# Second layer: seven block products for two f-tiles by two chunks of tokens, in place of eight

## The chip, the cores and the metric

The kernel runs on one core of a Trainium2 chip. The metric is device time in microseconds, from the profile's clock of one launch; the median of the runs is what counts. The engines are called as the profile calls them: PE (TensorE, matrix products), PEld (its weight loads), DVE (VectorE), ACT (ScalarE), POOL (GpSimd) and SP (SyncE, which only starts transfers here).

## What is computed

An attention in which a query sees the keys of its own hash bucket gives 1536 tokens of 512 values. Two feed-forward layers follow; the second one is what the change is about. The weights are float64 in memory, the activations float32.

```python
def _moe_ref(x, w1, w2, w3, w_out):            # first layer, d_ff 1024
    return ((x @ w1) * (x @ w2) @ w3) @ w_out

def _moe2_ref(x, w_gate, w_val, w_out):        # second layer, d_ff 1536
    gate = 1.0 / (1.0 + np.exp(-(x @ w_gate)))
    val = x @ w_val
    return (gate * val @ w_out).astype(np.float32)
```

## The kernel before

Attention, the decoding of the float64 weights and the first layer's first chunk fill the first 390 us or so. The rest is `moe` (L771). It works on tiles `(layer, chunk, f-tile)`: a chunk is 512 tokens (`CH`), of which there are three (`NSW`); an f-tile is 128 of the hidden values, 8 in the first layer (`NF1`), 12 in the second (`NF2`). The list `tiles` (L774) has the first layer's chunks two and three, then the second layer's chunks one, two and three.

Every product of float32 operands is made of three matmuls in a fast format: each operand is split into a high part, a rounded copy made by ACT, and a low part, the rest, made by a subtraction on DVE or POOL; `three` (L753) multiplies high by high, high by low and low by high into one bank of PSUM. `stage1` (L759) does so for the four blocks of 128 of the contraction, so a first product of a tile, `[128 hidden values x 512 tokens]`, is twelve matmuls into one bank.

For each tile:

- `weights` (L780) splits the gate's and the value's 512 x 128 block of weights, two tiles ahead: high parts on ACT, low parts on POOL (`split_w`, L741; tiles `wa`, `wb`).
- the first products go to the banks `pa` (gate) and `pb` (value), two of each.
- `post` (L788): ACT takes the sigmoid of `pa` into `a`, DVE multiplies `pb` by it in place, ACT and DVE split the result into `gh` and `gl`.
- `second` (L802), one tile late: the second product, twelve matmuls, adds to the four banks `m0` to `m3`, which hold 512 tokens by 512 outputs over all f-tiles of a chunk. At the chunk's end ACT (or DVE) copies the banks to `o` and SP stores them.

The operands that move through PE in the first products are the split activations: `xh`, `xl` for chunk one, and two pairs of tiles `x2_0_1`, `x2_1_1` (named `x` in the profile) for chunks two and three. The float32 weights of all f-tiles lie in SBUF, decoded, in `xall` and in the first layer's old tiles (`ftile`, L763). The float64 weights are decoded (`decode`, L136, on ACT, POOL and DVE) up to some 575 us.

The order of the instructions on each engine in `moe` comes from a scheduler that follows the code's priorities, with a wait for whoever wrote an operand or still reads a buffer.

Of the kernel before, what the change touches and what calls it, by code (L numbers as in the profile page):

```python
# [11 lines left out]
F32 = mybir.dt.float32  # L12
F32R = mybir.dt.float32r
# [5 lines left out]
AF = mybir.ActivationFunctionType  # L19
ALU = mybir.AluOpType  # L20
# [268 lines left out]
def lsh_attention_moe_moe2_kernel(  # L289
# [68 lines left out]
    wc = big.tile([P, NF1, DM], F32, name="wc")  # L358
# [377 lines left out]
    def split_x(s, t, kcs):  # L736
        for kc in kcs:
            act_copy(t[0][:, kc], xraw[s][:, kc])
            dve.tensor_tensor(out=t[1][:, kc], in0=xraw[s][:, kc], in1=f(t[0][:, kc]), op=ALU.subtract)

    def split_w(pl, nm, src, bufs=2, eng=pool):  # L741
        hi = pl.tile([P, DM], F32R, tag=nm + "h", name=nm + "h", bufs=bufs)
        lo = pl.tile([P, DM], F32R, tag=nm + "l", name=nm + "l", bufs=bufs)
        shp = src.shape
        h3, l3 = hi, lo
        if len(shp) == 3:
            h3 = hi.rearrange("p (k f) -> p k f", k=shp[1])
            l3 = lo.rearrange("p (k f) -> p k f", k=shp[1])
        act_copy(h3, src)
        eng.tensor_tensor(out=l3, in0=src, in1=f(h3), op=ALU.subtract)  # L750
        return hi, lo

    def three(ps, lhs, rhs, start, stop):  # L753

        for n, (x, y) in enumerate(((0, 0), (0, 1), (1, 0))):
            mm = pe.matmul(ps, lhsT=lhs[x], rhs=rhs[y], start=start and n == 0, stop=stop and n == 2)  # L756
        return mm

    def stage1(ps, w, x, kcs):  # L759
        for kc in kcs:  # L760
            three(ps, [t[:, kc * P:(kc + 1) * P] for t in w], [t[:, kc] for t in x], kc == 0, kc == KC - 1)

    def ftile(fi):  # L763

        ck, o = divmod(fi, KC)
        g = xall[:, o, ck * CH:(ck + 1) * CH].rearrange("p (k f) -> p k f", k=KC)
        if fi < NF1:
            return g, late["w1"][fi], late["w2"][fi].rearrange("p k f -> p (k f)")
        return g, wc[:, fi - NF1].rearrange("p (k f) -> p k f", k=KC), wc[:, fi - NF1 + KC]

    def moe(psM):  # L771
# [15 lines left out]

        def post(n, ps):  # L788
            m, s, fi = tiles[n]
            a = mp.tile([P, CH], F32, tag="a", name="a", bufs=2)  # L790
            if m == 1:
                act_copy(a, ps[0])
            else:
                act.activation(out=a, in_=ps[0], func=AF.Sigmoid)
            gl = mw.tile([P, CH], F32R, tag="gl0", name="gl", bufs=2)
            dve.tensor_tensor(out=ps[1], in0=ps[1], in1=a, op=ALU.mult)  # L796
            gh = mw.tile([P, CH], F32R, tag="gh0", name="gh", bufs=2)
            act_copy(gh, ps[1])
            late["gl"] = dve.tensor_tensor(out=gl, in0=ps[1], in1=f(gh), op=ALU.subtract).ins
            return gh, gl  # L800

        def second(n, g, wt, acc):  # L802
            m, s, fi = tiles[n]
            nf = NF1 if m == 1 else NF2
            last = n == len(tiles) - 1
            mm = None
            for c in range(4):
                cs = slice(c * P, (c + 1) * P)
                with tc.issue_after(mm.ins) if last and c else nullcontext():
                    if m == 1:  # L810
                        mm = three(acc[c], [t[:, cs] for t in wt], g, fi == 0, fi == nf - 1)
                    else:
                        mm = three(acc[c], [t[:, cs] for t in g], wt, fi == 0, fi == nf - 1)
            if fi < nf - 1:
                return
            for c in range(4):
                if m == 1:
                    act_copy(x2[s][0][:, c], acc[c])
                    dve.tensor_tensor(out=x2[s][1][:, c], in0=acc[c], in1=f(x2[s][0][:, c]), op=ALU.subtract)
                else:  # L820
                    o = mp.tile([P, DM], F32, tag="a" if last and c < 2 else "o", name="o", bufs=2)
                    if last and c % 2:
                        dve.tensor_copy(o, acc[c])
                    else:
                        act_copy(o, acc[c])
                    b, n = divmod(s * (CH // P) + c, NT)
                    sync.dma_start(out=out[b * S:(b + 1) * S].rearrange("(p c) d -> c p d", c=NT)[n], in_=o)
# [4 lines left out]
        for n in range(len(tiles) + 1):
            if n < len(tiles):
                ps = [psM.tile([P, 512], F32, tag=t, name=t) for t in ("pa", "pb")]
                x = x2[tiles[n][1]]
                w = ops.pop(n)
                for kcs in ([range(KC)] if n else [range(KC - 1), range(KC - 1, KC)]):
                    for i in range(2):
                        stage1(ps[i], w[i], x, kcs)
                m, s, fi = tiles[n]  # L840
                wts[n] = split_w(mp, "wt", wc[:, fi] if m == 1 else ftile(fi)[2], eng=dve)
                gs[n] = post(n, ps)
            if n == 0:
                continue
            if acc is None:
                acc = [psT.tile([P, 512], F32, tag="t", name="m0"), psT.tile([P, 512], F32, tag="t", name="m1"),
                       psT.tile([P, 512], F32, tag="t", name="m2"), psT.tile([P, 512], F32, tag="t", name="m3")]
            second(n - 1, gs.pop(n - 1), wts.pop(n - 1), acc)
# [15 lines left out]
    o = D // 2  # L864
# [12 lines left out]
    for r, c in ((slice(0, D), 0), (slice(D, P), o)):  # L877
        hi, lo = (t[r, c:c + NB] for t in pq)
# [43 lines left out]
    done = [0, 0.0]  # L922
# [85 lines left out]
```

## Time and profile before

| | |
|---|---|
| runs | 804.04, 804.48, 806.04 us (median 804.48) |
| profiled execution | 806.79 us; span of its instructions 805.0 us |
| granted clock of PE | 0.998 on average over the span |
| PE busy | 781.3 us, 97% of the span, 4016 matmuls |
| PEld | 661.1 us (82%) |
| DVE, ACT, POOL busy | 470.9 us (59%), 511.4 us (64%), 434.2 us (54%) |

A line of a group names the source line, engine, operation, output and inputs, shapes and how often, then the busy time and the mean of one. The line of a helper stands for all its callers (`act_copy` is L335). The chain of waits is the sequence of work that ended last, followed back from the last instruction. "Idle before" is how long the engine stood still in front of an instruction, with what released it behind the arrow.

### The profile page before, as it was taken

How to read it: one execution, taken by the hardware profiler on the slowest of the kernel's cores; microseconds unless marked ns; L12 is line 12 of the kernel's file. 1: busy time of each engine (PE TensorE's matmuls, PEld its weight loads, DVE VectorE, ACT ScalarE, POOL GpSimd, SP SyncE). 2: the span in 40 equal slices, each digit the busy share in tenths (PEclk: the TensorE clock that was granted, in tenths of full speed). 3: DMA queues.
4: the chain of work that ended last, by engine and by line, in shares of the span. 5: the costliest groups of instructions: out<-in, count | busy, mean ns of one | idle time of the engine just before them, and what ended most of it. 6: DMA issues, size and time to landing. Idle time of an engine off the chain costs nothing.

```text
span 805.0 us, 11532 instructions
## 1 busy us (share of the span) xinstructions
PE 781.3 (97%) x4016; PEld 661.1 (82%) x4016; DVE 470.9 (59%) x722; ACT 511.4 (64%) x946; POOL 434.2 (54%) x459
## 2 busy tenths in 40 slices
PE   6899899999899999999999999999999999999998
PEld 4789798899788899988888888888888888888886
DVE  6989988876997889782654445664422222222222
ACT  6889997877998888873555557766434333343332
POOL 6758886655675654494455557767423233332320
PEclk9999999999999999999999999999999999999999
DMA  9956676544366543230031213433001000010001
GB/s 278 223 160 151 187 197 180 145 123 117 117 163 167 135 126 102 69 106 0 27 105 53 79 53 116 141 110 105 0 1 53 0 1 1 0 53 1 0 1 53
DMA packets 28505, 74.46 MB, mean 92 GB/s; under 512 B 6048, under 2 KB 8352, under 8 KB 28448
## 3 DMA queue, kind: packets, MB, share of 16 engines
q1 hardware_dynamic: 28368, 73.73, 31.8%
q8 instruction: 32, 0.52, 0.3%
q14 instruction: 25, 0.20, 0.1%
q10 hardware_dynamic: 80, 0.00, 0.0%
HBM read 52.82 MB, written 3.19 MB: 70 GB/s over the span
## 4 chain that ended last, share of the span: by engine, by line
PE 84%; ACT 7%; POOL 3%; DVE 2%; issue 2%; DMA 2%; SPq 0%; ACTq 0%; POOLq 0%; DVEq 0%
PE m L756 18%; PE pa L756 18%; PE pb L756 18%; PE av L596 6%; PE tp L578 5%; PE p L756 5%; PE wacc L651 4%; PE s L526 3%; PE s L529 3%; PE y L756 2%; ACT e L545 2%; ACT pt L581 2%; PE gps L447 2%; DMA st<-in_moe_w_dram 1%; DVE sm L535 1%
## 5 line engine op out<-in xcount | busy, mean ns | idle before, releaser
L796 DVE TENSOR_TENSOR pb<-pb,a 128x512 f32<-128x512 f32 x52 | 36.3, 699 | 178.4 <-PE pb L756 178.4
L750 POOL TENSOR_TENSOR wal<-xall,wah 128x512 fp32r<-128x512 f32 x36 | 46.9, 1304 | 107.4 <-ACT wah L335 107.4
L583 DVE TENSOR_TENSOR pt<-tp,pt 128x512 fp32r<-128x512 f32 x144 | 94.9, 682 | 9.6 <-ACT pt L581 8.8
L578 PE MATMUL tp<-idf,e 128*128 128x128 f32 x576 | 95.8, 274 | 4.8 <-ACT e L545 2.3
L756 PE MATMUL pa<-x,wah 128*128 128x512 f32 x320 | 99.8, 391 | 0.0
L756 PE MATMUL pb<-x,wbh 128*128 128x512 f32 x320 | 98.8, 389 | 0.0
L398 POOL TENSOR_SCALAR dr<-st 128x512 bf16<-128x512 f32 x76 | 72.9, 971 | 45.8 <-issue 21.2
L535 DVE TENSOR_REDUCE sm<-s 128x1 f32<-128x768 f32 x96 | 90.3, 948 | 12.1 <-PE s L529 10.1
L545 ACT ACTIVATE e<-s,sm 128x768 f32<-128x768 f32 x96 | 86.7, 906 | 10.5 <-DVE sm L535 8.5
L581 ACT ACTIVATE pt<-tp 128x512 fp32r<-128x512 f32 x144 | 82.7, 599 | 9.3 <-PE tp L578 7.6
L578 PEld LDWEIGHTS tp<-idf,e 128*128 128x128 f32 x576 | 71.7, 141 | 15.7 <-ACT e L545 3.4
L596 PE MATMUL av<-pt,spv 128*128 128x256 f32 x576 | 80.3, 286 | 2.1 <-DVE pt L583 1.3
L596 PEld LDWEIGHTS av<-pt,spv 128*128 128x128 f32 x576 | 74.5, 190 | 5.2 <-DVE pt L583 2.5
L756 PEld LDWEIGHTS pa<-x,wah 128*128 128x128 f32 x320 | 60.1, 188 | 13.5
L756 PEld LDWEIGHTS pb<-x,wbh 128*128 128x128 f32 x320 | 60.1, 188 | 12.7
L399 POOL TENSOR_SCALAR da<-da 128x512 f32<-128x512 f32 x76 | 49.8, 663 | 37.2 <-ACT da L396 33.6
L526 PE MATMUL s<-bk,bq 128*128 128x384 f32 x192 | 61.2, 376 | 5.3 <-ACT e L545 4.9
L651 PE MATMUL wacc<-wo,t 128*128 128x512 f32 x192 | 61.9, 410 | 1.2 <-POOL wo L646 0.9
L756 PE MATMUL pa<-x,wal 128*128 128x512 f32 x160 | 62.4, 390 | 0.0
L756 PE MATMUL pb<-x,wbl 128*128 128x512 f32 x160 | 62.3, 389 | 0.0
L397 ACT ACTIVATE dr<-st 128x512 int16<-128x512 uint32 x76 | 60.1, 794 | 0.0
L529 PE MATMUL s<-ak,aq 128*128 128x384 f32 x192 | 58.7, 366 | 0.0
(146 smaller groups left out, 1823.2 us busy)
## 6 DMA issues: line engine op xcount, KB each, us to landing
st<-in_moe_w_dram SPq DMA_DIRECT2D x32, 512.0 KB, 5.3
st<-in_moe_w_out_dram SPq DMA_DIRECT2D x20, 512.0 KB, 4.4
st<-in_moe_w_gate_dram SPq DMA_DIRECT2D x12, 512.0 KB, 3.2
st<-in_moe_w_val_dram SPq DMA_DIRECT2D x12, 512.0 KB, 3.3
qk<-in_qk_dram SPq DMA_DIRECT2D x15, 384.0 KB, 4.5
rawv<-in_v_dram SPq DMA_DIRECT2D x16, 192.0 KB, 2.7
rr<-row SPq DMA_DIRECT2D x16, 192.0 KB, 3.7
out_dram<-o SPq DMA_DIRECT2D x12, 256.0 KB, 2.1
```

What stands on the lines that cost most here:

```text
L397: act.activation(out=r.bitcast(I16)[:, 0::2], in_=lw, func=AF.Copy, scale=2.0 ** -29)
L398: pool.tensor_scalar(out=r.bitcast(BF16)[:, 1::2], in0=f(hw), scalar1=0.0, scalar2=1.0, op0=ALU.mult, op1=ALU.mult)
L526: pe.matmul(s[:, half, :HS], lhsT=m["bq"][:, qs], rhs=m["bk"][:, ks], start=True, stop=False)
L529: pe.matmul(s[:, half, :HS], lhsT=m["aq"][:, qs], rhs=m["ak"][:, ks], start=False, stop=True)
L535: dve.tensor_reduce(out=b, in_=s[:, :, :HS], op=ALU.max, axis=AX.XY, negate=True)
L545: act.activation(out=e.rearrange("p (a c) -> p a c", a=2), in_=s[:, :, :HS], func=AF.Exp, bias=sm, scale=1.0, accum_out=su_t[h][:, t:t + 1],)
L578: pe.transpose(ps[:, i * P:(i + 1) * P], e_t[g - g % 2 + a][:, c * P:(c + 1) * P], idf)
L581: act.activation(out=dh, in_=src, func=AF.Copy)
L583: dve.tensor_tensor(out=d, in0=src, in1=f(dh), op=ALU.subtract)
L596: pe.matmul(acc[:w.shape[1], :2 * P].rearrange("p (a t) -> p a t", a=2), lhsT=w, rhs=r[:, :, c], start=(c == 0 and i == 0), stop=(c == NT ...
L651: pe.matmul(acc, lhsT=t3[x][:, j], rhs=wo[y][:, j], start=(j == 0 and n == 0), stop=(j == NF1 - 1 and n == 2))
L756: mm = pe.matmul(ps, lhsT=lhs[x], rhs=rhs[y], start=start and n == 0, stop=stop and n == 2)
```

## The change

Chunk one of the second layer stays as it is. Its chunks two and three, which were 24 tiles one behind another, are done together, two f-tiles at a time (six pairs, `pair`).

For a pair, the weights of a side (gate or value) are taken as two rows (f-tiles) by two halves of the contraction, A11, A12, A21, A22, and the activations as two halves of the contraction by two chunks, B11 (lower half, chunk two), B21 (upper half, chunk two), B12 and B22 (chunk three). The four results, f-tile by chunk, would be eight block products of six matmuls. `seven` makes them of seven products with sums of blocks:

- S1 = A21 + A22, S2 = S1 - A11, S3 = A11 - A21, S4 = A12 - S2, made for each pair and side on DVE (`sums`), split by ACT and POOL;
- T1 = B12 - B11, T2 = B22 - T1, T3 = B22 - B12, T4 = B21 - T2, made once (`blocks`), as are the splits of the B blocks;
- the products A11 x B11, S2 x T2, S1 x T1, S3 x T3, A12 x B21, A22 x T4 and S4 x B22, in four banks (two `pa`, two `pb`), with one copy on ACT (`s1`) and seven additions on DVE, some in place in a bank, one (c22) to SBUF.

The gate's results are then passed through the sigmoid, and the value's are multiplied by them. Chunk two's product is split and goes into its second product in the next pair. Chunk three's is stored in SBUF where the gate's weights of the pair had been; its second products, twelve groups of twelve matmuls, follow after all pairs, with banks `npa`, `npb`.

The first layer's second product for chunks two and three is copied to float32 tiles `xf` first, since the blocks are sums of them; T3 and T4 take the place of chunk one's `xh` and `xl` after its last tile.

```diff
-        tiles = [...] + [(2, s, fi) for s in range(NSW) for fi in range(NF2)]
+        tiles = [...] + [(2, 0, fi) for fi in range(NF2)]
...
             for c in range(4):
                 if m == 1:
-                    act_copy(x2[s][0][:, c], acc[c])
-                    dve.tensor_tensor(out=x2[s][1][:, c], in0=acc[c], in1=f(x2[s][0][:, c]), op=ALU.subtract)
+                    if c == 0:
+                        xf[s] = [mw.tile([P, CH], F32, tag="wh" if s == 1 else "wl", name=f"xf{s}", bufs=3) for _ in range(3)]
...
+                    act_copy(xf[s][c], acc[c])
...
+        def sums(w, tiles4, half):
+            lo, up = slice(0, 2), slice(2, 4)
+            w0, w1 = w
...
+            def split(h, l, x):
+                act_copy(h, x)
+                pool.tensor_tensor(out=l, in0=x, in1=f(h), op=ALU.subtract)
+
+            tmp = xt["f"][:, 2 * half:2 * half + 2].rearrange("p k (j f) -> p (k j) f", f=P)
+            S1, S2, S3, S4 = [tmp[:, 2 * i:2 * i + 2] for i in range(4)]
+            split(h0, l0, w0)
+            dve.tensor_tensor(out=S1, in0=w1[:, lo], in1=w1[:, up], op=ALU.add)
+            dve.tensor_tensor(out=S2, in0=S1, in1=w0[:, lo], op=ALU.subtract)
+            dve.tensor_tensor(out=S3, in0=w0[:, lo], in1=w1[:, lo], op=ALU.subtract)
+            dve.tensor_tensor(out=S4, in0=w0[:, up], in1=S2, op=ALU.subtract)
+            split(h2, l2, tmp[:, 2:6])
+            split(h1[:, up], l1[:, up], S1)
+            split(h1[:, lo], l1[:, lo], w1[:, up])
+            split(h3, l3, S4)
...
+        def product(ps, w, x):
+            for k in range(2):
+                three(ps, [t[:, k] for t in w], [t[:, k] for t in x], k == 0, k == 1)
+
+        def seven(w, c22, done):
+            pa, pb, pc, pd = [psM.tile([P, 512], F32, tag=t, name=t) for t in ("pa", "pb", "pa", "pb")]
...
+            add = lambda o, x, y: dve.tensor_tensor(out=o, in0=x, in1=y, op=ALU.add)
+            product(pa, w["A11"], xs["B11"])
+            act_copy(s1, pa)
+            product(pb, w["S2"], xs["T2"])
+            add(u2, pb, s1)
+            product(pc, w["S1"], xs["T1"])
+            add(u5, pc, u2)
+            product(pd, w["S3"], xs["T3"])
+            add(u3, pd, u2)
+            add(c22, pc, u3)
+            product(pa, w["A12"], xs["B21"])
+            add(pa, pa, s1)
+            done(0, 0, pa)
+            done(1, 1, c22)
+            product(pb, w["A22"], xs["T4"])
+            add(pb, pb, u3)
+            done(1, 0, pb)
+            product(pc, w["S4"], xs["B22"])
+            add(pc, pc, u5)
+            done(0, 1, pc)
+
+        def pair():
...
+            for q in range(NF2 // 2):
...
+                def gates(r, c, x):
+                    fi = 2 * q + r
+                    gate[r, c] = t = flat(ftile(fi)[0]) if c else mp.tile([P, CH], F32, tag="a", name="a", bufs=2)
+                    act.activation(out=t, in_=x, func=AF.Sigmoid)
+
+                def values(r, c, x):
+                    if c:
+                        dve.tensor_tensor(out=gate[r, c], in0=x, in1=gate[r, c], op=ALU.mult)
+                        return
+                    dve.tensor_tensor(out=x, in0=x, in1=gate[r, c], op=ALU.mult)
...
+                    act_copy(gh, x)
+                    dve.tensor_tensor(out=gl, in0=x, in1=f(gh), op=ALU.subtract)
...
+                seven(wa_next[0], flat(ftile(2 * q + 1)[0]), gates)
+                if q + 1 < NF2 // 2:
+                    wa_next[0] = sums_a(q + 1)
...
+                    add_second(acc, [(g_last[r], w_last[r]) for r in range(2)], 2 * q - 2)
+                w_last = [wt(2 * q + r) for r in range(2)]
+                seven(wb, flat(ftile(2 * q + 1)[1]), values)
+                if q + 1 < NF2 // 2:
+                    wb = sums_b(q + 1)
+                g_last = g
...
+            ready = [(stored(fi), wt(fi)) for fi in range(2)]
+            for fi in range(NF2):
+                add_second(acc, [ready.pop(0)], fi, fi == NF2 - 1)
+                if fi + 2 < NF2:
+                    ready.append((stored(fi + 2), wt(fi + 2)))
```

How it moves instructions, at two places. On PE, chunks two and three before: the end of one tile's second product (banks `m`) and the next tile's gate product, moving tiles `x_0_1` and `x_1_1`, weights `wah`, `wal`.

```order
L756 MATMUL m_4807<-wth,gh 128x512
L756 MATMUL m_4807<-wtl,gh 128x512
L756 MATMUL m_4807<-wth,gl 128x512
L756 MATMUL pa<-x_0_1_4702,wah 128x512
L756 MATMUL pa<-x_1_1_4703,wah 128x512
L756 MATMUL pa<-x_0_1_4702,wal 128x512
L756 MATMUL pa<-x_0_1_4702,wah 128x512
L756 MATMUL pa<-x_1_1_4703,wah 128x512
L756 MATMUL pa<-x_0_1_4702,wal 128x512
L756 MATMUL pa<-x_0_1_4702,wah 128x512
L756 MATMUL pa<-x_1_1_4703,wah 128x512
L756 MATMUL pa<-x_0_1_4702,wal 128x512
```

On PE now, where one pair ends and the next begins: S2 x T2 of the next gate (moving tile `xs`, weights `swh`), S4 x B22 of the value (moving tile `xsx_0_2`, weights `swbh`), and the second products of chunk two that follow.

```order
L756 MATMUL pb<-xs,swh 128x512 x2
L756 MATMUL pb<-xs,swl 128x512
L756 MATMUL pb<-xs,swh 128x512 x2
L756 MATMUL pb<-xs,swl 128x512
L756 MATMUL pa<-xsx_0_2_6148,swbh 128x512 x2
L756 MATMUL pa<-xsx_0_2_6148,swbl 128x512
L756 MATMUL pa<-xsx_0_2_6148,swbh 128x512 x2
L756 MATMUL pa<-xsx_0_2_6148,swbl 128x512
L756 MATMUL m_4804<-wth,gh 128x512
L756 MATMUL m_4804<-wtl,gh 128x512
L756 MATMUL m_4805<-wth,gh 128x512
L756 MATMUL m_4805<-wtl,gh 128x512
```

A bank is now filled by six matmuls in place of twelve; the second product of a tile is no longer in one piece but takes `gh` first, and the next `pa` product stands between it and its `gl` part.

On DVE, chunks two and three before: three operations for each tile, the multiplication by the gate (L796), the low part of the product (L799) and that of the output weights (L750).

```order
L799 TENSOR_TENSOR gl_7306<-pb_7275,gh_7308 128x512
L750 TENSOR_TENSOR wtl_7358<-wc_80,wth_7357 128x512
L796 TENSOR_TENSOR pb_7332<-pb_7332,a_7361 128x512
L799 TENSOR_TENSOR gl_7363<-pb_7332,gh_7365 128x512
L750 TENSOR_TENSOR wtl_7415<-w2r0_2575,wth_7414 128x512
L796 TENSOR_TENSOR pb_7389<-pb_7389,a_7418 128x512
L799 TENSOR_TENSOR gl_7420<-pb_7389,gh_7422 128x512
L750 TENSOR_TENSOR wtl_7484<-w2r1_2576,wth_7483 128x512
```

On DVE now, in the value's seven products of one pair (`u2`, `u3`, `u5`, the c22 sum in `w1r7`; L926 the additions, L975 and L977 the multiplications, L981 `gl`, L891 and L893 sums of weights for a later pair).

```order
L926 TENSOR_TENSOR u2_7524<-pb_7520,s1_7523 128x512
L926 TENSOR_TENSOR u5_7526<-pa_7521,u2_7524 128x512
L926 TENSOR_TENSOR u3_7525<-pb_7522,u2_7524 128x512
L893 TENSOR_TENSOR xsx2_1_2_6230<-wc_80 128x256
L926 TENSOR_TENSOR pa_7519<-pa_7519,s1_7523 128x512
L926 TENSOR_TENSOR w1r7_2574<-pa_7521,u3_7525 128x512
L977 TENSOR_TENSOR pa_7519<-pa_7519,a_7446 128x512
L926 TENSOR_TENSOR pb_7520<-pb_7520,u3_7525 128x512
L975 TENSOR_TENSOR xall_79<-w1r7_2574,xall_79 128x512
L891 TENSOR_TENSOR xsx2_1_2_6230<-wc_80 128x256
L977 TENSOR_TENSOR pb_7520<-pb_7520,a_7456 128x512
L981 TENSOR_TENSOR gl_7565<-pa_7519,gh_7564 128x512
```

Between the multiplication of the bank `pa` (L977) and its low part `gl` four other operations stand on this queue, among them two whose operands are all in SBUF, L975 and L891.

## Rows read from the trace of the kernel before

**Rows 1.** Chain in order of time, 500 to 805 us: start us, us, what.
```profile
by line: PE m L756 34.0%; PE pb L756 32.4%; PE pa L756 32.4%; DVE o L823 0.2%; issue 0.0%
...
591.75 2.81 PE pa L756 x12
594.56 2.79 PE pb L756 x12
597.35 2.79 PE m L756 x12
600.14 2.75 PE pa L756 x12
602.89 2.72 PE pb L756 x12
605.61 2.81 PE m L756 x12
608.42 2.73 PE pa L756 x12
...
792.87 2.72 PE pb L756 x12
795.59 5.63 PE m L756 x24
801.22 0.02 issue
801.25 0.69 DVE o L823
```

**Rows 2.** Windows: busy us (xcount) of PE, PEld, DVE, ACT, POOL, then PEclk.
```profile
600.14:801.25 201.11, 201.07 (x877) 164.22 (x875) 50.71 (x74) 74.65 (x126) 56.94 (x44) 1.00 0.03 12
550.20:558.60 8.40, 8.40 (x37) 6.74 (x36) 4.40 (x8) 5.38 (x10) 5.97 (x6) 1.00 0.34 125
```

**Rows 3.** Groups by form, DVE: xcount | busy us, mean ns | idle before.
```profile
L796 DVE TENSOR_TENSOR pb<-pb,a 128x512 f32<-128x512 f32 x52 | 36.3, 699 | 178.4 <-PE pb L756 178.4
...
L609 DVE TENSOR_TENSOR xall<-av,xall 64x256 f32<-64x256 f32 x48 | 19.8, 413 | 7.1 <-ACT xall L335 6.4
```

**Rows 4.** Timeline of DVE, two operations back to back: start us, us.
```profile
506.29 0.69 DVE L819 TENSOR_TENSOR x<-m,x 128x512 fp32r<-128x512 f32 x1 [0.56 <-ACT x L335]
506.90 0.68 DVE L799 TENSOR_TENSOR gl<-pb,gh 128x512 fp32r<-128x512 f32 x1
```

**Rows 5.** Groups by form, ACT.
```profile
L335 ACT ACTIVATE gh<-pb 128x512 fp32r<-128x512 f32 x52 | 31.1, 599 | 21.3 <-DVE pb L796 21.2
L335 ACT ACTIVATE wah<-xall 128x512 fp32r<-128x512 f32 x36 | 22.6, 628 | 45.5 <-PE pa L756 45.5
...
L335 ACT ACTIVATE xall<-av 64x256 f32<-64x256 f32 x48 | 18.3, 381 | 12.8 <-PE av L596 12.1
```

**Rows 6.** Groups by form, POOL.
```profile
L750 POOL TENSOR_TENSOR wal<-xall,wah 128x512 fp32r<-128x512 f32 x36 | 46.9, 1304 | 107.4 <-ACT wah L335 107.4
L465 POOL TENSOR_TENSOR bq<-qk,aq 128x384 fp32r<-128x384 f32 x30 | 31.2, 1045 | 1.7
```

**Rows 7.** Timeline of all engines in one tile of chunk two.
```profile
638.26 0.39 PE L756 MATMUL pb<-x,wbl 128*128 128x512 f32 x1
...
638.75 0.70 DVE L796 TENSOR_TENSOR pb<-pb,a 128x512 f32<-128x512 f32 x1 [4.09 <-PE pb L756]
...
639.48 0.60 ACT L335 ACTIVATE gh<-pb 128x512 fp32r<-128x512 f32 x1 [0.33 <-DVE pb L796]
...
640.11 0.69 DVE L799 TENSOR_TENSOR gl<-pb,gh 128x512 fp32r<-128x512 f32 x1 [0.67 <-ACT gh L335]
```

**Rows 8.** Timeline of all engines where TensorE waits for ACT.
```profile
203.53 0.92 ACT L545 ACTIVATE e<-s,sm 128x768 f32<-128x768 f32 x1
...
204.59 0.14 PEld L578 LDWEIGHTS tp<-idf,e 128*128 128x128 f32 x1 [0.81 <-ACT e L545]
```

**Rows 9.** Line L733, DVE, operands in SBUF: ns min/median/max, starts.
```profile
L733 DVE TENSOR_TENSOR xl<-xall,xh x4: 677/1228/1771, 387.0 to 393.8; 128x512 fp32r<-128x512 f32 x4
```

More of the change, by code (lines that the diff above doesn't have):

```diff
@@ L771, in moe @@
     def moe(psM):
-        tiles = [(1, s, fi) for s in range(1, NSW) for fi in range(NF1)] + [(2, s, fi) for s in range(NSW) for fi in range(NF2)]
+        tiles = [(1, s, fi) for s in range(1, NSW) for fi in range(NF1)] + [(2, 0, fi) for fi in range(NF2)]
         mp, mw = late["mp"], late["mw"]
@@ L804, in second @@
             nf = NF1 if m == 1 else NF2
-            last = n == len(tiles) - 1
-            mm = None
             for c in range(4):
                 cs = slice(c * P, (c + 1) * P)
[L809 to L813, printed above, removed]
+                if m == 1:
+                    three(acc[c], [t[:, cs] for t in wt], g, fi == 0, fi == nf - 1)
+                else:
+                    three(acc[c], [t[:, cs] for t in g], wt, fi == 0, fi == nf - 1)
             if fi < nf - 1:
@@ L817, in second @@
                 if m == 1:
-                    act_copy(x2[s][0][:, c], acc[c])
-                    dve.tensor_tensor(out=x2[s][1][:, c], in0=acc[c], in1=f(x2[s][0][:, c]), op=ALU.subtract)
-                else:
[L821 to L827, printed above, removed]
+                    if c == 0:
+                        xf[s] = [mw.tile([P, CH], F32, tag="wh" if s == 1 else "wl", name=f"xf{s}", bufs=3) for _ in range(3)]
+                        xf[s].append(mw.tile([P, CH], F32, tag="a0", name="xf1") if s == 1 else mp.tile([P, CH], F32, name="xf2"))
@@ new lines, in second, with store @@
+                    act_copy(xf[s][c], acc[c])
+                else:
+                    store(s, c, acc[c])
+        def store(s, c, ps, last=False):
+            o = mp.tile([P, DM], F32, tag="a" if last and c < 2 else "o", name="o", bufs=2)
+            if last and c % 2:
+                dve.tensor_copy(o, ps)
+            else:
+                act_copy(o, ps)
+            b, n = divmod(s * (CH // P) + c, NT)
+            sync.dma_start(out=out[b * S:(b + 1) * S].rearrange("(p c) d -> c p d", c=NT)[n], in_=o)
@@ new lines, in banks, with lows, blocks @@
+        def banks():
+            return [psT.tile([P, 512], F32, tag="t", name=f"m{i}") for i in range(4)]
+        xs, xf, xt = {}, {}, {}
+        def lows(nm, hi, lo, src):
+            for k in range(2):
+                act_copy(hi[:, k], src[k])
+                dve.tensor_tensor(out=lo[:, k], in0=src[k], in1=f(hi[:, k]), op=ALU.subtract)
+            xs[nm] = (hi, lo)
+        def blocks(n):
+            step = n - 2 * NF1
+            lo, up = slice(0, 2), slice(2, 4)
+            sub = lambda o, x, y: dve.tensor_tensor(out=o, in0=x, in1=y, op=ALU.subtract)
+            full = lambda nm, dt: mp.tile([P, KC, CH], dt, tag=nm, name="xs" + nm)
+            if step == 1:
+                xt["a"] = [full("x2_0_1", F32R), full("x2_1_1", F32R)]
+                lows("B11", *[t[:, lo] for t in xt["a"]], xf[1][:2])
+            if step == 2:
+                lows("B21", *[t[:, up] for t in xt["a"]], xf[1][2:])
+            if step == 3:
+                t = full("x2_0_2", F32R)
+                lows("B22", t[:, lo], t[:, up], xf[2][2:])
+            if step == 4:
+                xt["f"] = full("x2_1_2", F32)
+                for k in range(2):
+                    sub(xt["f"][:, k], xf[2][k], xf[1][k])
+            if step == 5:
+                for k in range(2):
+                    sub(xt["f"][:, 2 + k], xf[2][2 + k], xt["f"][:, k])
+            if step == 9:
+                for nm, tag, k in (("T1", "da", 0), ("T2", "dr", 2)):
+                    lows(nm, *[pl.tile([P, 2, CH], F32R, tag="st", name="xs", bufs=2) for pl in ((mp, mp) if k else (dec, dec))],
+                         [xt["f"][:, k + j] for j in range(2)])
+                t3, t4 = [[mp.tile([P, CH], F32, tag=tag, name="x" + tag, bufs=2) for _ in range(2)] for tag in ("da", "dr")]
+                for k in range(2):
+                    sub(t4[k], xf[1][2 + k], xt["f"][:, 2 + k])
+                    sub(t3[k], xf[2][2 + k], xf[2][k])
+                xt["t"] = t3, t4
+            if step == NF2:
+                for nm, r, t in (("T3", lo, xt["t"][0]), ("T4", up, xt["t"][1])):
+                    lows(nm, *[x[:, r] for x in x2[0]], t)
@@ new lines, in sums @@
+        def sums(w, tiles4, half):
+            lo, up = slice(0, 2), slice(2, 4)
+            w0, w1 = w
+            (h0, l0), (h1, l1), (h2, l2), (h3, l3) = [[t.rearrange("p (k f) -> p k f", f=P) for t in x] for x in tiles4]
+            def split(h, l, x):
[12 more added lines that the diff above has]
+            split(h3, l3, S4)
+            return {"A11": (h0[:, lo], l0[:, lo]), "A12": (h0[:, up], l0[:, up]), "A22": (h1[:, lo], l1[:, lo]), "S1": (h1[:, up], l1[:, up]),
+                    "S2": (h2[:, lo], l2[:, lo]), "S3": (h2[:, up], l2[:, up]), "S4": (h3, l3)}
@@ new lines, in sums_a, with sums_b @@
+        def sums_a(q):
+            t = lambda tag: mw.tile([P, DM], F32R, tag=tag, name="s" + tag, bufs=3)
+            ts = [(t("wh"), t("wl")) for _ in range(3)]
+            x = mw.tile([P, DM], F32R, tag="a0", name="sa0")
+            ts.append((x[:, :2 * P], x[:, 2 * P:]))
+            return sums([ftile(2 * q + i)[0] for i in range(2)], ts, 0)
+        def sums_b(q):
+            t = lambda tag: mp.tile([P, DM], F32R, tag=tag, name="s" + tag, bufs=2)
+            ts = [(t(x + "h"), t(x + "l")) for x in ("wa", "wa", "wb")]
+            h, l = t("wbh"), t("wbl")
+            ts.append((h[:, :2 * P], l[:, :2 * P]))
+            return sums([ftile(2 * q + i)[1] for i in range(2)], ts, 1)
@@ L831, in moe @@
         acc = None
[L832 to L842, printed above, removed]
+        wa_next, acc1 = [None], [None]
+        for n in range(len(tiles)):
+            ps = [psM.tile([P, 512], F32, tag=t, name=t) for t in ("pa", "pb")]
+            x = x2[tiles[n][1]]
+            w = ops.pop(n)
+            for kcs in ([range(KC)] if n else [range(KC - 1), range(KC - 1, KC)]):
+                for i in range(2):
+                    stage1(ps[i], w[i], x, kcs)
+            m, s, fi = tiles[n]
+            wts[n] = split_w(mp, "wt", wc[:, fi] if m == 1 else ftile(fi)[2], eng=dve)
+            gs[n] = post(n, ps)
             if n == 0:
                 continue
[L845 to L848, printed above, removed]
+            if n == 1:
+                acc1[0] = banks()
+            second(n - 1, gs.pop(n - 1), wts.pop(n - 1), acc1[0])
             with tc.issue_after(late["gl"]):
@@ L855, in moe @@
                 split_x(2, x2[2], range(KC))
+            blocks(n)
+            if n == len(tiles) - 2:
+                wa_next[0] = sums_a(0)
+        blocks(len(tiles))
+        pair()
     def decodes(n):
```

36 lines of the change are left out of this document (added).

## The prediction

> **What bounds the kernel now.** I read the chain of waits first, in order of time, over the last 305 us. From 600.14 us to 801.22 us it is TensorE alone [rows 1]: a gate group of twelve matmuls (`pa`, 2.75 or 2.73 us), a value group (`pb`, 2.72), a second-product group (`m`, 2.81), and again, 8.26 us for a tile. These are the 24 tiles of chunks two and three, and one more `m` group for chunk one's last tile: 24 x 8.26 + 2.81 = 201.05 us against the 201.08 of the stretch. Then the table of windows: in that stretch TensorE is busy 201.07 of 201.11 us at a granted clock of 1.00 (the upper of its two levels, 2.4 GHz), DVE 50.71, ACT 74.65, POOL 56.94 [rows 2]. So fewer matmuls here end the kernel earlier one for one, as long as the engines that feed and empty them keep up.
>
> **What is removed.** Chunks two and three lose 12 of 96 first-product matmuls for each pair of f-tiles: two sides (gate, value) of seven products of six matmuls, 84, instead of 96. Six pairs: 504 instead of 576, 72 fewer.
>
> What one costs is known within limits. In chunks two and three twelve take 2.73 or 2.72 us, 0.227 each; in chunk one, with the moving tiles `xh` and `xl`, 2.81 (0.234), as in every `m` group [rows 1]. Of the seven products, those on B11, B21 and B22 move the old `x2` buffers, and S3 x T3 and A22 x T4 move `xh` and `xl`; T1 and T2 are in new buffers, and the gate's weights are in other buffers than now. I take the middle, 0.231; the ends are 0.227 and 0.234.
> Before: 24 x (2.73 + 2.72) = 130.8 us. After: 504 x 0.231 = 116.4. **Gain 14.4 us** (16.4 at 0.227, 12.9 at 0.234). The 25 `m` groups stay, at 2.81. A pair then takes 84 x 0.231 + 2.81 x 2 = 25.0 us of TensorE, and chunk three's second products follow as twelve groups, 33.7 us, behind all pairs.
>
> **What is added, off TensorE.** Prices: DVE 0.70 us for 512 columns, 0.41 for 256 (a 64-partition row is nearest) [rows 3], 0.61 apart where one does not need the other [rows 4]; ACT 0.60 and 0.63, 0.38 for 256 [rows 5]; POOL 1.30 for 512, and for 256 two thirds of the 384-column 1.05, 0.70 [rows 6].
> For one pair:
> - DVE: 14 additions, 4 multiplications, 2 low parts of the product, 2 of the output weights (22 of 512 columns), 8 sums of weights (256): 22 x 0.70 + 8 x 0.41 = 18.7 us, 16.7 with the 0.61.
> - ACT: 2 copies of the first product, 4 sigmoids, 2 + 2 high parts, 4 weight splits of 512 and 6 of 256: 14 x 0.63 + 6 x 0.38 = 11.1 us.
> - POOL: 4 x 1.30 + 6 x 0.70 = 9.4 us.
>
> All are below 25.0, so cost nothing as sums. The cover is TensorE's 25.0; DVE has 6.3 to 8.3 us of it left. No DMA is added or moved: SP's list of loads and stores is in the same order, chunk two's stores only wait for the end of the pairs.
>
> **Whether each bank is handed over in time.** There are four banks for first products and seven products use them, so TensorE now waits for additions. I walk one pair from the end of the gate's A12 x B21 (time 0). A product takes 1.39. DVE or ACT starts 0.26 after the next matmul could issue (last `pb` matmul 638.26, plus 0.23, DVE at 638.75 [rows 7]); ACT's result is in TensorE 0.14 later (204.45 to 204.59 [rows 8]).
> - Gate's S4 x B22 is issued at 2.77. Its bank is free when c22 is added: DVE does the A12 bank 0.26 to 0.96 and c22 to 1.56. Spare 1.2.
> - Value's S1 x T1 at 6.93 needs that bank read by the sigmoid: product over at 4.16, DVE 4.42 to 5.12, ACT to 5.75. Spare 1.1.
> - Value's S4 x B22 at 12.47 needs value's c22. S1 x T1 is over at 8.31, u5 to 9.27, u3 9.87, a sum of weights and the A12 addition to 10.8, c22 11.4. Spare 1.0.
> - Next gate's A11 x B11, at 15.73 behind eight second-product matmuls, needs the bank that the value's A11 and A12 shared, so the low part `gl`. On DVE: multiplication to 12.0, the A22 addition 12.6, the c22 multiplication, which meets POOL's weight splits, to 13.65, a sum of weights 13.95, multiplication 14.6, `gl` 15.2. **Spare 0.5, the tightest place.**
> - The others (both S3 x T3, S2 x T2, the copies of the first product) have 1.2 us or more.
>
> So a pair runs without a stall if a delay of 0.5 us there does not come. In the last pair nothing stands between A22 x T4 and S4 x B22, so TensorE waits for c22: 11.32 - 11.08 = 0.24 us. The bound below is no stall at all (a stall cannot be negative); the one above is in the rivals. I take 0.24 and 0.25 for each of six pairs, 1.7 us, nearer to the walk than to its failure.
>
> **What moves into chunk one.** Splits of B11 to B22 and of T1 to T4, and the first sums of weights, run while chunk one's tiles are on TensorE. A tile of 8.40 us has DVE busy 4.40, ACT 5.38, POOL 5.97 [rows 2]. The largest step adds to DVE four low parts, four differences and four sums: 8 x 0.61 + 4 x 0.41 = 6.5 us, 2.5 over the tile, once. It is hidden since second products come a tile late: `pb` is over at 638.49, `gl` at 640.80 [rows 7], its first use at 638.49 + 2.81 + 5.45 = 646.75, 5.9 us to spare. T3 and T4 overwrite `xh` and `xl` after chunk one's last `pb`: four ACT copies and four DVE low parts, about 4 us; S3 x T3 comes 8.2 us after that `pb`. I take nothing; were this cover gone it would be 2.5 us once.
>
> The tail after the last matmul (copies, stores) keeps its operations. In chunk three's 33.7 us each group of 2.81 needs two ACT copies (1.26) and two DVE low parts (1.4): hidden; once not, DVE and ACT in turn would cost 1.3 us at most per group.
>
> **Sum.** 14.4 - 1.7 = 12.7 us. The profiled execution took 806.79 us (span 805.0), so 794.1; it lies 2.3 above the median of the runs, 804.48, which goes to **791.8**.
>
> **A rule against this.** A DVE operation whose operands are all in SBUF is 0.68 us at best and 1.77 at worst in one row of four, median 1.23 [rows 9]: it waits up to 1.09 us. Each pair has eleven such (the sums, two output-weight parts, the c22 multiplication) beside ten POOL operations; their own time is in the sum above at its best value, and the tightest place has two of them. With no waits the gain is 14.4 less 0.24; with the full wait twice at the tightest place it is the first rival.
> The Trainium skill (SBUF — State Buffer, SBUF: two separate sides) says that a DVE operation with two SBUF inputs and a GpSimd operation that reads SBUF take a shared port pair in turn, whole instructions at a time, the other blocked. The row agrees: the longest exceeds the shortest by less than one POOL operation.
>
> **Rivals.**
> - *The waits break the tightest handover.* c22's multiplication and the sum behind it each wait 1.09; I had 0.55 in the walk: 2 x 1.09 - 0.55 - 0.5 = 1.1 us of stall per pair, 6.8 over six. Gain 14.4 - 0.24 - 6.8 = 7.4: **797.1**. For it: POOL's splits of A11, A12 and S1 stand exactly there. Against: POOL is busy 9.4 of 25.0, so two full waits at this place in every pair are unlikely. Chance 0.15.
> - *DVE becomes the bound, and the kernel slower.* With all eleven waiting w each, DVE needs 18.7 + 11 w. It passes TensorE's 25.0 from w = 0.57, and what was saved (2.4 us a pair) is gone from w = 0.79. At 1.09 it is 30.7: 6 x 5.7 - 14.4 = 19.8 us slower, **824.3**. For it: the median of [rows 9] has 0.55. Against: nineteen of the thirty DVE operations of a pair read or write a PSUM bank, and those keep 0.70 [rows 3]; while DVE does one of them POOL's operation goes by. Chance 0.06.
> - *No change*: stalls of 2.4 us a pair, between these two, 804.5. Chance 0.04.
> - That the change does not do what it says is out: the list of TensorE's instructions has 72 matmuls fewer.
>
> **How the numbers follow.** The forecast, 791.8, has 0.75; its own ends are 0.227 with no stall (16.4: 788.1) and 0.234 with the 1.7 doubled (12.9 - 3.4 = 9.5: 795.0). The range reaches on to the first rival and somewhat over it, 788.0 to 798.5, and leaves out the two last cases and tails. About 0.3%, 2.4 us, can be told from no change: faster 0.75 + 0.15 = 0.90, same 0.04, slower 0.06.
>
> **What would show it.** Matmuls 3944 instead of 4016 at the same clock; pairs about 25.0 us apart; groups of six between 1.36 and 1.41 us; TensorE's waits in the pairs at `pa` on DVE's `gl` (L981), each below 0.5 us. Wrong would be: waits over 1 us there or at c22 (the first rival); DVE above nine tenths in the pairs (the second); idle TensorE before the first pair (chunk one's cover); TensorE at 1.2 GHz.

## The result, and the profile after

The changed kernel takes **791.41 us** (median; runs from 790.84 to 793.98), the kernel before 804.26 beside it: ratio 0.9843, 95% interval 0.9816 to 0.9869, so 1.6% faster, clear of the noise of the runs. The forecast was 791.8.

The profiled execution took 791.21 us. Its page:

```profile
span 788.9 us, 11559 instructions
PE 766.2 (97%) x3944; PEld 647.7 (82%) x3944; DVE 562.3 (71%) x868; ACT 521.6 (66%) x984; POOL 440.9 (56%) x471
```

72 matmuls fewer, DVE at 71% in place of 59. The chain of waits, in order of time (start us, us, what), from the first product of the pairs on:

```profile
598.03 1.40 PE pa L756 x6
...
620.30 1.36 PE pa L756 x6
621.66 1.87 PE m L756 x8
623.53 1.41 PE pa L756 x6
...
645.34 1.36 PE pa L756 x6
646.71 1.87 PE m L756 x8
648.57 1.41 PE pa L756 x6
...
744.15 1.64 PE pa L756 x6
745.78 5.61 PE m L756 x24
...
785.15 0.02 issue
785.17 0.69 DVE o L825
```

It is TensorE alone again: products of six between 1.36 and 1.41 us, S4 x B22 of one pair to that of the next 25.04 us. The stretch from the first product to the end of the last second product is 785.15 - 598.03 = **187.12 us**, where it was 201.08 [rows 1]: 13.96 less. One product is longer, that at 744.15 in the last pair (1.64, where the others take 1.36 to 1.41). The windows of that stretch, of two pairs and of chunk three's second products (columns: window and us; then busy us, count, of PE, PEld, DVE, ACT, POOL; then the granted clock):

```profile
598.03:785.15 187.12, 187.10 (x805) 150.69 (x803) 120.48 (x195) 77.61 (x145) 48.53 (x50) 1.00 0.04 13
645.34:670.40 25.06, 25.06 (x110) 20.30 (x109) 18.30 (x31) 10.56 (x20) 9.64 (x11) 1.00 0.00 1
670.40:695.45 25.05, 25.05 (x109) 20.29 (x109) 18.39 (x31) 10.56 (x20) 9.68 (x11) 1.00 0.00 1
751.39:785.15 33.76, 33.74 (x145) 26.78 (x143) 15.03 (x23) 14.93 (x27) 0.00 (x0) 1.00 0.10 39
```

Against [rows 2], TensorE is full at the same clock of 1.00 and DVE does 120.48 us in place of 50.71. A pair has 18.3 us of DVE under 25.05 of TensorE.

Ahead of the stretch, too, something differs: it begins at 598.03 and not at 600.14. That is not the change. The last sixteen `y` matmuls of the first layer's first chunk start at 382.25 here and at 384.38 before, and from there to the first product it is 215.78 us here and 215.76 before, TensorE busy throughout:

```profile
382.25:598.03 215.78, 215.78 (x931) 174.69 (x931) 132.29 (x193) 132.69 (x228) 136.78 (x124) 1.00 0.22 74
```

Up to that place PE, DVE, ACT and POOL run the same instructions in the same order in both traces. So the 2 us are a difference between two executions ahead of it; the profiled execution of before lay 2.5 us above its own median. Below I compare stretches (first product of the pairs to the last matmul), which are free of that, beside the medians.

The tightest handover of the walk, next gate's A11 x B11 behind the value's `gl`, in the timeline (start us, us, engine):

```profile
645.13 1.23 DVE L975 TENSOR_TENSOR xall<-w1r,xall 128x512 f32<-128x512 f32 x1
646.29 0.41 DVE L891 TENSOR_TENSOR xsx<-w1r 128x256 f32<-128x256 f32 x1
646.62 0.69 DVE L977 TENSOR_TENSOR pb<-pb,a 128x512 f32<-128x512 f32 x1
647.23 0.68 DVE L981 TENSOR_TENSOR gl<-pa,gh 128x512 fp32r<-128x512 f32 x1
...
648.18 0.39 PE L756 MATMUL m<-wtl,gh 128*128 128x512 f32 x1
648.41 0.63 PE L756 MATMUL pa<-xsx,swh 128*128 128x512 f32 x2
```

c22's multiplication (L975) takes 1.23 where 0.68 is its least; `gl` is over at 647.91, and the matmul starts at 648.41 without a wait: 0.5 us to spare. In the last pair nothing stands between A22 x T4 and S4 x B22 to cover c22 (`wc` here):

```profile
743.39 0.68 DVE L926 TENSOR_TENSOR wc<-pa,u 128x512 f32<-128x512 f32 x1
...
744.12 0.30 PEld L756 LDWEIGHTS pa<-xsx,swbh 128*128 128x128 f32 x2 [0.41 <-DVE wc L926]
744.13 0.73 PE L756 MATMUL pa<-xsx,swbh 128*128 128x512 f32 x2
```

TensorE waits until 744.13; that is the longer product of the chain, the only stall in the pairs. The last matmul of A22 x T4 started at 743.75, so the next could have been issued at 743.98, 0.23 later: 0.15 us of waiting. Another 0.10 is lost behind the wait, since the two matmuls there take 0.73 in place of 0.63.

### The profile page after: what moved, and what is told of

Its sections match the earlier page's. It is cut to its first block, busy times and chain, and to the rows that moved or that the text cites. A ratio compares the mean times of both kernels' runs of the same rounds, so it can differ in the third digit from the quotient of the medians.

```text
span 788.9 us, 11559 instructions
## 1 busy us (share of the span) xinstructions
PE 766.2 (97%) x3944; PEld 647.7 (82%) x3944; DVE 562.3 (71%) x868; ACT 521.6 (66%) x984; POOL 440.9 (56%) x471
## 4 chain that ended last, share of the span: by engine, by line
PE 85%; ACT 4%; POOL 4%; DMA 3%; issue 2%; DVE 2%; SPq 0%; POOLq 0%; ACTq 0%; DVEq 0%
PE pa L756 18%; PE pb L756 16%; PE m L756 14%; PE av L596 6%; PE tp L578 5%; PE wacc L651 5%; PE p L756 4%; PE s L526 3%; PE s L529 3%; PE y L756 2%; DMA st<-in_moe_w_dram 2%; PE npb L756 2%; PE npa L756 2%; PE gps L447 2%; ACT e L545 1%
## 5 line engine op out<-in xcount | busy, mean ns | idle before, releaser
L396 ACT ACTIVATE da<-st 128x512 f32<-128x512 f32 x76 | 51.2, 674 | 15.9 <-DVE w1r L405 6.9
L796 DVE TENSOR_TENSOR pb<-pb,a 128x512 f32<-128x512 f32 x28 | 19.4, 696 | 57.5 <-PE pb L756 53.2
L526 PEld LDWEIGHTS s<-bk,bq 128*128 128x128 f32 x192 | 35.3, 195 | 11.8 <-ACT e L545 7.4
L400 DVE TENSOR_SCALAR da<-da 128x512 uint32<-128x512 uint32 x76 | 39.4, 533 | 6.7 <-POOL da L399 6.5
L756 PE MATMUL pa<-x,wah 128*128 128x512 f32 x128 | 40.4, 393 | 0.0
L651 PEld LDWEIGHTS wacc<-wo,t 128*128 128x128 f32 x192 | 34.4, 188 | 6.7 <-POOL wo L646 1.6
L756 PE MATMUL pb<-x,wbh 128*128 128x512 f32 x128 | 39.7, 390 | 0.0
L756 PE MATMUL m<-wth,gh 128*128 128x512 f32 x96 | 38.0, 396 | 0.0
```

What stands on the lines that cost most here:

```text
L526: pe.matmul(s[:, half, :HS], lhsT=m["bq"][:, qs], rhs=m["bk"][:, ks], start=True, stop=False)
L651: pe.matmul(acc, lhsT=t3[x][:, j], rhs=wo[y][:, j], start=(j == 0 and n == 0), stop=(j == NF1 - 1 and n == 2))
```

## The experiments

**Theory**: the time is TensorE's matmuls and their price; what was added on DVE, ACT and POOL is hidden, with 0.5 us to spare at one handover. **Rivals**: the gain comes from the order in pairs, not from the seven products; the spare is used up by waits (the first rival), or larger than thought; DVE is near its limit (the second rival).

### Eight products in the pairs

The order in pairs and the late second products of chunk three stay; the seven products become eight, and the sums, additions and copies that the seven need go with them (B12 is kept under T1's name). From the kernel's edit:

```diff
...
-            product(pa, w["A11"], xs["B11"])
-            act_copy(s1, pa)
-            product(pb, w["S2"], xs["T2"])
-            add(u2, pb, s1)
...
+            for i, (r, c, ps) in enumerate(((0, 0, pa), (1, 1, pb), (1, 0, pc), (0, 1, pd))):
+                for h in range(2):
+                    for k in range(2):
+                        x = xs[(("B11", "B21"), ("T1", "B22"))[c][h]]
+                        wt = w[(("A11", "A12"), ("A21", "A22"))[r][h]]
+                        three(ps, [t[:, k] for t in wt], [t[:, k] for t in x], h == k == 0, h == k == 1)
+                done(r, c, ps)
```

> The pairs as in the change, but each side by eight block products of six matmuls (B12 takes T1's place, A21 that of S1; no sums S1 to S4, no additions, no copy of the first product). Theory (the gain is the 72 matmuls and nothing else): 72 x 0.231 = 16.6 us more on TensorE, less the 0.26 us stall of the last pair: about 16.3 above the changed kernel's 791.4, so 807.7 (807 to 808.5). Rival (part of the gain comes from how the work is ordered in pairs, or chunk three's second products behind them): clearly below 807, down to 791. Rival (the sums and additions themselves cost time that this kernel gets back): below 807 as well, with TensorE's idle time smaller by as much.

Measured: **807.07 us**; against the kernel before 1.0029 (1.0004 to 1.0054). Chain of this kernel:

```profile
596.61 2.81 PE pa L756 x12
...
638.45 2.76 PE pa L756 x12
641.21 2.80 PE pb L756 x12
...
660.70 5.61 PE m L756 x24
666.32 2.76 PE pa L756 x12
...
800.88 0.02 issue
```

A pair takes 666.32 - 638.45 = 27.87 us, 2.82 more than with seven. The stretch is 204.27 us (596.61 to 800.88), 17.15 over the changed kernel's. (16.3 was expected; the removed matmuls alone are 6 x 2.82 = 16.9.) So the order in pairs gains nothing by itself. It even costs: 204.27 is 3.2 us more than before's 201.08 with as many matmuls. A stall among chunk three's second products is some 0.5 of it (0.42 of waiting at 772.50, and a slower start); the other 2.7 are the price of a matmul, (27.87 - 5.61) / 96 = 0.232 here against the 0.227 of [rows 1]. The operands lie in other buffers; that this is the cause is shown in part by the last experiment.

### One and two reads more of the bank at the tight handover

DVE copies the bank once or twice more behind `gl`, in the first five pairs, so that it comes free later. An order put on TensorE holds S1 x T1, S3 x T3 and the rest of the second products behind A11 x B11, so that it stays where it stood, behind the first eight second-product matmuls. The loop that makes the copies (twice in the second kernel):

```diff
...
                     dve.tensor_tensor(out=gl, in0=x, in1=f(gh), op=ALU.subtract)
+                    for _ in range(1 if r == 0 and q + 1 < NF2 // 2 else 0):
+                        dve.tensor_copy(gate[r, c], x)
```

> At five of the six handovers to the next gate, DVE reads the bank once more behind gl (one copy of 512 columns); A11 x B11 is held at its place in TensorE's order. In the changed kernel gl is over at 647.91 and the matmul begins at 648.41: spare 0.5. The copy ends at 648.50, TensorE sees it 0.14 later: 0.2 us of stall, five times: 1.0 us, so 792.4 (791.4 to 793.4). Rival (TensorE is not bound to that handover so closely, spare of 1 us or more): 791.4, no wait of pa on DVE. Rival (waits on SBUF eat the spare already): about 0.6 x 5 = 3 us or more, 794.5.

> As with one copy, but two of them; the second stands behind the S4 addition and the second gl on DVE, which end at 649.4 in the changed kernel, 650.0 with the first copy, so the bank is free at 650.65. TensorE's A11 x B11 would begin at 648.41: stall 2.4 us, five times: 12 us, 803.3 (799 to 805), nearly all of the gain given back, with the waits of pa on DVE in the pairs. Rival (the tightest handover is not there or is looser by far): below 796.

Measured: 791.43 us with one copy, **801.59** with two. With one, the medians tell nothing, the chain does:

```profile
671.52 1.87 PE m L972 x8
673.39 1.65 PE pa L756 x6
...
696.81 1.87 PE m L972 x8
```

The product takes 1.65 in place of 1.41, and the pair 696.81 - 671.52 = 25.29 in place of 25.05: 0.24 us, expected 0.2. TensorE stands still for 0.15 of it (the matmul starts at 673.37 in place of 673.22); the other 0.1 is the slower first matmul behind a wait. Four of the five handovers have it; the fifth has none: there c22's multiplication is issued 0.09 us ahead of POOL's operation (720.39 and 720.48) and takes 0.68, and no sum of weights follows it. The stretch is 0.92 us longer (188.04), expected 1.0; the spread of runs hides so little. With two, the waits of TensorE in the pairs (us in all, times, the longest):

```profile
PE pa L756 <- DVE a L994: 9.2, 5, 2.1
```

Five waits, 2.1 us the longest, on the second copy (`a`), and a stretch 10.30 us longer (expected 12; the fifth wait was only 0.75 us). So 0.6 us more on the bank is just over the spare, and 1.2 us more, with what stands between on DVE's queue, gives back some three quarters of the gain. The rival of a looser handover falls, and so does that of a spare already used up.

### The low parts of the weights on DVE, and three times over

```diff
             def split(h, l, x):
                 act_copy(h, x)
-                pool.tensor_tensor(out=l, in0=x, in1=f(h), op=ALU.subtract)
+                dve.tensor_tensor(out=l, in0=x, in1=f(h), op=ALU.subtract)
```

The second kernel makes each of these subtractions three times.

> The low parts of the weights of the pairs go from POOL to DVE: DVE has 18.2 us a pair now, and gets 4 x 0.61 to 0.68 and 6 x 0.35 to 0.41 more, less the waits for POOL (some 1.5 us): 21.2 to 23.4 of 25.05; POOL does nothing there. Theory (below 25 DVE's load as a sum costs nothing, a handover that slips by one or two operations costs up to 1.3 us a pair): 791.4 to 798. Rival (DVE is close to its limit already, or its waits are not idle time that can be used): 800 and more. SBUF-only operations (L975, L891 to L894) should all take their shortest time, 0.68 and 0.41, with POOL idle.

> Rival 2 by dose: the low parts of the pairs' weights on DVE as in the run before (there 20.9 us of DVE per pair, period 25.09), each now made three times over: per pair 8 more operations of 512 columns (0.61) and 12 of 256 (0.35), 9.1 us, DVE some 29.5 to 30 a pair. Theory (DVE's sum costs nothing below TensorE's 25.05 and sets the period above it): periods of about 29.5 in the four or five pairs whose successor's weights are made beside them, 4.5 x 5 = 22 us over the run before (796.1), 818 (813 to 825), TensorE waiting for DVE. Rival (the handovers slip far more than the sum, since each waits in DVE's order): 830 and more. Rival (DVE has more room than its busy time says): below 805.

Measured: **796.11 us** for one, **810.43** for three (1.0075 of before, 1.0049 to 1.0100). The first lies in its range (791.4 to 798), the second below its own (813 to 825). Windows of two pairs with the low parts once:

```profile
672.13:697.20 25.07, 25.07 (x110) 20.32 (x109) 20.89 (x40) 10.45 (x20) 0.00 (x0) 1.00 0.00 1
697.20:722.30 25.10, 25.10 (x110) 20.32 (x110) 19.21 (x35) 10.70 (x20) 0.00 (x0) 1.00 0.00 1
```

Three times over:

```profile
658.29:688.07 29.78, 27.04 (x110) 19.59 (x108) 29.78 (x63) 10.54 (x20) 0.00 (x0) 1.00 0.00 0
688.07:716.54 28.47, 26.31 (x109) 19.70 (x108) 28.47 (x59) 10.91 (x20) 0.00 (x0) 1.00 0.00 1
716.54:744.99 28.45, 26.39 (x109) 19.80 (x108) 28.45 (x59) 10.91 (x20) 0.00 (x0) 1.00 0.00 1
```

With DVE at 20.9 us the pairs stay at 25.1. In the second kernel DVE is busy in all of a pair and is the period: from S4 x B22 to S4 x B22 it takes 29.09, 29.78, 28.47 and 28.45 us, 28.95 on average (the first from 629.20 to 658.29). Expected was 29.5. The operations cost what I took: they stand 0.60 us (512 columns) and 0.33 (256) apart without a gap. Most of the miss is that I counted five such periods, 4.5 us longer each; there are four, 3.9 longer, and the one into the last pair, beside which no more weights are made, is not lengthened. The 4.3 us by which the first kernel's stretch is longer are not in the pairs shown. They are three waits, one at 647.04 us ahead of a second product and two in the last pair (751.50 and 754.59):

```profile
PE m L756 <- ACT gh L335: 2.6, 2, 1.4
PE pa L756 <- DVE wc L926: 1.2, 1, 1.2
```

At 647.04 ACT makes two high parts of weights before the `gh` that TensorE waits for; in the last pair the operation waited for comes late in DVE's order. So DVE's load as a sum costs nothing at 20.9 of TensorE's 25 us; what costs is a late operation at a handover. The second rival is a true mechanism, and 18.3 us was far from it.

### The sums of weights on POOL

```diff
-            dve.tensor_tensor(out=S1, in0=w1[:, lo], in1=w1[:, up], op=ALU.add)
+            pool.tensor_tensor(out=S1, in0=w1[:, lo], in1=w1[:, up], op=ALU.add)
...
```

> The other way: the eight sums of weights of a pair go from DVE to POOL: DVE 18.3 less 8 operations, some 13 to 14 us, POOL 9.6 + 8 x 0.7 to 0.9, some 15 to 17 of 25.05. Theory (neither DVE's load nor its waits for POOL cost anything now): the pairs stay at 25.05 apart, 790 to 792.5. Rival (DVE's waits at the sums do cost a part of a pair): faster by 1 us or more. Rival (POOL, now the slower engine for a sum, is late with a split): stalls at S2 x T2 or S4 x B22, 793 and more.

Measured: 789.73 us (0.9830, 0.9807 to 0.9853). A pair:

```profile
668.79:693.82 25.03, 25.03 (x110) 20.29 (x108) 14.78 (x23) 10.34 (x20) 16.09 (x19) 1.00 0.01 1
```

25.03 us with DVE at 14.8 and POOL at 16.1. The stretch is 187.35, 0.2 longer: one new wait at the first pair. The median is 1.7 below the 791.41 of the change, as this run's rival of a gain would have it, but that is not the pairs' doing: the profiled execution reaches the stretch 1.7 us earlier (596.32), and the changed kernel run again took 789.95 (next experiment). Neither DVE's load nor its waits cost anything in the changed kernel. What the waits were shows c22's multiplication (L975: ns shortest/median/longest, starts), in the changed kernel, then with the low parts on DVE, then with the sums on POOL:

```profile
L975 DVE TENSOR_TENSOR xall<-w1r,xall x4: 1140/1228/1239, 620.1 to 695.2; 128x512 f32<-128x512 f32 x4
```

```profile
L975 DVE TENSOR_TENSOR xall<-w1r,xall x4: 681/683/685, 623.3 to 700.8; 128x512 f32<-128x512 f32 x4
```

```profile
L975 DVE TENSOR_TENSOR xall<-w1r,xall x4: 681/681/701, 618.9 to 693.6; 128x512 f32<-128x512 f32 x4
```

With POOL silent in the pairs the 0.55 us of waiting is gone. In the last kernel POOL is busier, and it is gone as well; the timelines say why. In the changed kernel POOL's operation runs from 645.07 to 645.81, and DVE's, issued at 645.13, ends 0.55 after it:

```profile
645.07 0.74 POOL L886 TENSOR_TENSOR swal<-w1r,swah 128x256 fp32r<-128x256 f32 x1
```

With the sums on POOL, DVE's comes first (643.56 to 644.24), and POOL's, begun within it, is the one that takes longer:

```profile
643.65 1.19 POOL L886 TENSOR_TENSOR swal<-w1r,swah 128x256 fp32r<-128x256 f32 x1
```

Whichever is issued later ends 0.55 to 0.60 us behind the other's end, most of its own time alone (0.68 and 0.74): it waits for the other. The changed kernel has both cases: in its fifth pair DVE's operation is issued at 720.15 and takes 0.68, POOL's at 720.24 and takes 1.18. The Trainium skill (SBUF — State Buffer, SBUF: two separate sides) says it so, as a shared port pair taken in turn, and these rows agree.

### Operands of a matmul from one pool

The pitch of 0.227 or 0.234 went, in most groups of both kernels, with the pools of tiles, `mp` against `mw` and `dec`: lower where both operands lie in `mp`, or neither does. Two edits move operands: chunk three's `gh`, `gl` into `mp` beside `wth`, `wtl`; and the weights of the pairs dealt out by product.

```diff
...
             def stored(fi):
-                gh = mw.tile([P, CH], F32R, tag="gh0", name="gh", bufs=2)
-                gl = mw.tile([P, CH], F32R, tag="gl0", name="gl", bufs=2)
+                gh = mp.tile([P, CH], F32R, tag="wah", name="swah", bufs=2)
+                gl = mp.tile([P, CH], F32R, tag="wal", name="swal", bufs=2)
...
         def sums_b(q):
+            h2, l2 = r("wbh"), r("wbl")
+            ts = [(r("wbh"), r("wbl")), (t("wh"), t("wl")), (h2[:, :2 * P], l2[:, :2 * P]), half(t("wl")), (h2[:, 2 * P:], l2[:, 2 * P:])]
...
```

> The changed kernel once more, as the standard for the three beside it: 791.4 us (790.5 to 793).

> In chunk three's second products the split operand gh, gl lies in the buffers wah, wal (pool mp, where wth and wtl are) instead of gh0, gl0 (pool mw). Theory (a matmul takes 0.227 when both operands lie in the same of the two pools and 0.234 when they lie in different ones): 144 matmuls x 0.007 = 1.0 us less, groups of twelve at 2.73 in place of 2.81; 790.4 against 791.4. Rival (the pitch hangs on which tile moves, or on the bank, not on the pools): groups stay at 2.81, no change.

> The weights' buffers of the pairs are dealt out by product in place of by side: A11, A12, S2 and S4, which meet B11, B21, T2 and B22 in pool mp, go to mp; A22, S1 and S3, which meet T4, T1 and T3 in mw and dec, go to mw (the first gate stays as it was). By the pools 24 of the gate's matmuls (five pairs) and 18 of the value's (six pairs) change from 0.234 to 0.227: 228 x 0.007 = 1.6 us less, 789.8; groups of six all at 1.36 to 1.37. Rival (the pitch is not set by the pools): groups of 1.41 stay, 791.4. Against both: S2 and S3 are split apart, one operation more on ACT and POOL per side, and a handover may slip, by up to 1 us per pair.

> Both edits: 1.6 + 1.0 = 2.6 us less than the changed kernel, 788.8 (0.33%). Rival (pitch not set by the pools): 791.4.

| | median us | runs | stretch us |
|---|---|---|---|
| changed kernel again | 789.95 | 789.52 to 791.52 | 187.11 |
| second products of chunk three | 789.77 | 788.59 to 793.35 | 187.56 |
| weights of the pairs | 788.98 | 788.14 to 790.89 | 186.68 |
| both | **788.93** | 788.47 to 789.60 | 185.58 |

The last matmuls of the chain, in the changed kernel:

```profile
782.32 0.71 PE npa L756 x3
783.03 0.70 PE npb L756 x3
```

and with `gh`, `gl` in `mp`:

```profile
784.88 0.68 PE npa L756 x3
785.56 0.68 PE npb L756 x3
```

All of chunk three's second products went to 0.68 for three, 1.1 us in sum (1.0 expected). Alone the edit gains nothing: two new waits at `m` (1.0 us together) stand in the last pair. The new buffers let chunk three's first splits start early, and on DVE two of their low parts (L1005) now stand ahead of chunk two's `gl`, for which TensorE waits:

```profile
746.01 0.68 DVE L1005 TENSOR_TENSOR swal<-xall,swah 128x512 fp32r<-128x512 f32 x1
...
748.41 0.68 DVE L1005 TENSOR_TENSOR swal<-xall,swah 128x512 fp32r<-128x512 f32 x1
...
750.21 0.68 DVE L981 TENSOR_TENSOR gl<-pa,gh 128x512 fp32r<-128x512 f32 x1
```

With both edits these waits are gone. The edit on the pairs gave 0.4 of the 1.6 expected: many of its products still take 1.38 to 1.41. So the pool is not the whole rule there, and what else sets the pitch stays open. Both edits together shorten the stretch by 1.5 us (2.6 expected). The median of 788.93 us is 1.0 below the change's 789.95, less than the 0.3% that two medians can tell.

## Why the prediction was right

- **The matmuls removed.** Right. Predicted 14.4 us less 0.24 of stall, 14.16; the stretch has 13.96. A pair of 25.05 is 84 matmuls at 0.2313 and 24 at 0.234; I took 0.231. Eight products in the same order show the parts: 72 matmuls are worth some 17 us, and 2.7 go to the dearer price of those that stay. The middle price of 0.231 held the two in one number; it was a choice between two ends and not read from a row.
- **The work added on other engines.** Right: DVE 18.3 us a pair (16.7 to 18.7 predicted), ACT 10.6 (11.1), POOL 9.6 (9.4), all hidden. DVE could take 20.9 without a longer pair; at 28.5 and more it was the pair.
- **The handovers.** Right to the tenth at the tightest one: spare 0.5 predicted, 0.5 in the timeline, and a copy of 0.6 pitch turned it into a loss of 0.24. The stall of the last pair was foreseen with 0.24 and costs 0.25, but that agreement is luck: 0.15 is waiting, and 0.1 is the slower matmul behind it, which the walk did not have.
- **The allowance of 0.25 for each pair** was the one term too large, by 1.5 us: the pairs have no stall but the last one's. From 806.79 to 791.21 the profiled executions lie 15.58 us apart where 12.7 was forecast: 13.96 in the stretch, 2.1 ahead of it, and 0.5 the other way outside the span of instructions (806.79 - 805.0 = 1.8 us before, 791.21 - 788.9 = 2.3 after).
- **The hit to 0.4 us** is in part luck. The medians lie 12.9 and 13.4 us apart in the two comparisons, the stretches 13.96. Half a microsecond of that is the time outside the span: 2.3 us in each of the eight runs of the changed kernel, 1.8 to 1.9 in every run of the kernel before whose span is on record; the rest is within what executions of one kernel differ. So an allowance 1.5 too large met medians that show 1.1 less than the stretch.
- **What moved into chunk one.** Right: 215.78 against 215.76 us up to the first product.
- **The first rival** (waits break the tight handover) has its first half: c22's multiplication waited 0.55 us in four of six pairs, as much as the walk had allowed (in a fifth DVE's operation came 0.09 us ahead of POOL's), and the sum behind it in the pair shown not at all. It took one more copy of the bank for a stall.
- **The second rival** did not come about; forced, it gave 810.43, slower than before, by the mechanism that was priced.

## What to carry to other kernels

Where one engine is full, work taken off it counts one for one as long as each buffer is handed over in time: the sums of the other engines say little, the walk along the handovers says it, and the least spare is worth finding before the run. Price the matmuls that stay by the buffers they will read, not by those they read before. Compare stretches in the trace beside the medians: a fixed event ahead of the edit shows what part of a difference is another execution's.

## What the runs showed that I had not expected

- A wait of TensorE costs 0.1 us more than it lasts: two matmuls take 0.73 behind the wait at 744.13 and 0.63 at 648.41 without one. Each of the nine waits on the copies has it as well.
- A tile's pool moved a matmul's pitch by 3%: in chunk three's second products, in all 144 of them (0.234 to 0.227). In the pairs it did so only in part.
- Twice what cost time was not an engine's load but its order: a low part moved to DVE, or one that could start earlier, came ahead of an operation that TensorE was waiting for.
